# A fused retention and squared-ReLU kernel on one core: fixed rows of operations for each engine in place of a greedy list

## The chip, the cores and the metric

The kernel runs on one core of one Trainium2 chip. The metric is the device time of one execution in microseconds, given as the median of several runs of the same program. The profile is a separate look: one execution, recorded by the hardware profiler, whose span runs from the first to the last instruction. Engines are named as in the profile: PE (TensorE, matrix products; PEld is its loading of weights), DVE (VectorE), ACT (ScalarE), POOL (GpSimd) and SP (SyncE, which issues nearly all transfers).

## What is computed

```python
def _attn_ref(q, k, v):                       # 4 x 8 x 768 x 64 each, float32
    gamma = 1.0 - 2.0 ** (-5.0 - np.arange(H))
    for t in range(S):
        state = gamma * state + k_t (outer) v_t          # 64 x 64 for each batch and head
        y[:, :, t] = (1 / np.sqrt(D)) * (q_t @ state)

def _moe_ref(x, w_in, w_out):                 # x: y as 3072 tokens x 512
    h = np.maximum(x @ w_in, 0.0)             # 3072 x 2048
    return h * h @ w_out                      # 3072 x 512
```

A recurrence over 768 steps in 32 heads gives 3072 tokens of 512 numbers; a feed-forward layer with a squared ReLU follows.

## The kernel before

**Tiles.** The tokens are cut into 24 tiles of 128, six to a batch; tile m is the unit of everything below. Inside a tile the recurrence is done as two chunks of 64 with matrix products: scores of q and k under a mask, sums of k and v into the running state, values from the scores, and the state applied to q. The powers of gamma are folded into v beforehand and into the result afterwards. The inputs are float32, the products bfloat16.

**Operations.** The program is a list of named operations, each added by `pl.add` with its engine, a planned duration and what it reads and writes. The names are used throughout:

- `ldq`, `ldk`, `ldv` m: transfers of tile m, 256 KB each (512 KB for tiles 0 and 2, which are loaded as pairs), issued by SP (L537, L717). `ldwin0` to `ldwin3` are 512 KB pieces of w_in, `ldwin4`, `ldwin5` and `ldwout0` to `ldwout3` pieces of 1 MB (L910). The text calls the loads q9, k9, v9 and so on for short. Four buffers of each of q, k and v are held.
- `cq`, `ck`: casts to bfloat16, on DVE, ACT or POOL (L518 to L522). `cv`: the scaling of v (L728 on DVE, L553 for the pairs). `cwin`, `cwout`: casts of weight blocks.
- `X` m, from tile 7 on: a DMA transpose issued by SP (L761), which turns the cast q and k of the tile (`kqs`) into `qkT`. Earlier tiles are transposed on PE (`T`, evacuated by `E`).
- `A`, `B`, `C` (tiles 0 to 3, in pairs) and the visits `V` on PE. `V9.10` computes the values of tile 9 (L787, L802) and, in the same stretch, the scores and sums of tile 10 (L813, L824), so it needs X10 and the scaled v10. `P` (mask), `S` n.0 and n.1 (state) and `Y` (result into `xt`) are its operations on DVE.
- `F1` b.f on PE (L936): a group of products of block b, two tiles wide (one for b = 2 and 3), with part f of w_in, eight matmuls of 256 columns or sixteen of 128. `R` (ReLU, ACT, L943) empties its PSUM bank, `Q` (square, ACT or DVE, L950 and L952) writes `h`.
- `F2` t.j (L1108): the second layer for tiles 0 to 3, evacuated by `O` and stored by `st0` to `st3`. Tiles 4 to 23 take the second layer in pairs with seven products instead of eight, `M1` to `M7` (L1032), named by the first tile of the pair. DVE makes sums of blocks of h for them (L1007; `S1`, `S2`, `S5`, `S6`, `S7` before and `H1` to `H7` after the change) and of w_out (`WT`, L982); `e4`, `cc` on ACT (L1054, L1060) and `t`, `u`, `w`, `c` on DVE (L1050) read the products from two banks; `st4.0`, `st4.1` and so on store them (L1084, 256 KB each).

**Buffers that tie them.** Four PSUM banks `fps` are shared by F1, F2, M and T; two more pairs (`sc`, `yy`) serve the visits. R and Q share two buffers. Three output buffers (`osb`) and one more (`wu`) pass from store to store, so a result can be written only when the store before it from the same buffer has landed.

**What sets the order.** `Plan.schedule` (L68) runs when the program is built. It keeps a planned clock for every engine, the PSUM banks, the DMA stream and the fetching of instructions, and places one operation at a time: of all that are ready, the one that can start earliest, then the one with the lowest priority number (`prio`, overridden by the table `RANK`, L316). Operations that several engines could do go to the one that could start first, unless the table `HOME` (L277) says which. The sequence that comes out is emitted in order of planned start, so that each engine's instructions have a fixed order on the chip; waits between engines are semaphores that the framework adds. The order of the loads is a priority too (`ORDER`, L340). PE begins with 20 tiny matmuls and, in gaps before 20 us of the plan, gets fill matmuls (`ident`), 36 in all, that keep it busy while it waits.

The lines that choose:

```python
key = (t, o["prio"], i)
if best is None or key < best[0]:
    best = (key, i, eng)
```

Of the kernel before, what the change touches and what calls it, by code (L numbers as in the profile page):

```python
# [11 lines left out]
BF16 = mybir.dt.bfloat16  # L12
# [6 lines left out]
class Plan:  # L19
# [14 lines left out]
    HOP = 0.15  # L34

# [5 lines left out]
    def add(self, name, eng, dur, reads=(), writes=(), fn=None, prio=0.0, lat=0.0, bank=None, after=(), count=0, slot=None, lock=()):  # L41
# [22 lines left out]
        self.ops.append(dict(i=i, name=name, eng=eng, flex=flex, deps=sorted(deps), fn=fn,  # L64
                             prio=prio, lat=lat, bank=bank, count=count, slot=slot, lock=lock))
        return i

    def schedule(self, nbanks, max_open, nslots):  # L68
# [12 lines left out]
        for o in ops:  # L81
            for e in o["eng"]:
                eng_free.setdefault(e, 0.0)
                pool.setdefault(e, set())
                if left[o["i"]] == 0:
                    pool[e].add(o["i"])
# [15 lines left out]
        while done < n:  # L102
            best = None
            for eng, cand in pool.items():
                ef = eng_free[eng]
                for i in cand:
# [21 lines left out]
            (t, _, _), i, eng = best  # L128
            o = ops[i]
            for e in o["eng"]:  # L130
                pool[e].discard(i)
# [34 lines left out]
            else:  # L166
                if eng == "PE":
# [21 lines left out]
                    if any(before < x <= issued for x in range(self.BLOCK0 - self.AHEAD, issued + 1, self.BLOCK)):  # L189
# [14 lines left out]
                end[i] = t + dur + o["lat"]  # L204
# [15 lines left out]
            for u in users[i]:  # L220
                same = list(ops[u]["eng"]) == [eng] and not move
                ready_at[u] = max(ready_at[u], start[i] + dur if same else end[i] + self.HOP)
                left[u] -= 1
                if left[u] == 0:
                    for e in ops[u]["eng"]:
                        pool[e].add(u)
# [11 lines left out]
AHEAD = 4  # L238
WARM = 20.0
FILL = 0.215  # L240
WARMING = 18.4
PACE = 8
LEAD = 2
# [5 lines left out]
CVT = {'DVE': 0.69, 'POOL': 1.07}  # L249
TCAST = {'DVE': 0.43, 'ACT': 0.63, 'POOL': 0.64}  # L250
TEVAC = {'ACT': 0.6, 'DVE': 0.62}
NPAIR = 2
F2LAG = 3.5
F2WAIT = 4
LAST = [256, 128, 128]
CAST = {"k": {"DVE": 0.43, "ACT": 0.63, "POOL": 0.64}, "q": {"DVE": 0.43, "ACT": 0.63, "POOL": 0.64}}
WCAST = {"DVE": 0.43, "ACT": 0.63, "POOL": 0.64}
EVAC = {"ACT": 0.6, "DVE": 0.62}
WPRIO = {"in": -2.0, "out": 2.0, "sum": 3.0}
# [3 lines left out]
SQUARE = {"DVE": 0.7, "ACT": 0.63}  # L263
WSUM = {"DVE": 0.69}
ASUM = {"DVE": 0.69}
LAGS = {
    16: 4.0, 4: 10.75, 6: 18.25, 10: 2.25, 20: 1.75, 14: 3.0, 8: 2.25, 18: 3.0, 12: 1.75, 22: 2.0,
}
RELU = {"ACT": 0.6}
# [4 lines left out]
PAIRS_A = {"S1": ((0, 0), (1, 1), ALU.add, None), "S5": ((0, 0), (0, 1), ALU.add, None),  # L274
           "S2": ((1, 0), (1, 1), ALU.add, None), "S6": ((1, 0), (0, 0), ALU.subtract, (1, 0)),
           "S7": ((0, 1), (1, 1), ALU.subtract, (0, 1))}
HOME = {  # L277
# [36 lines left out]
}  # L314
ROUND = []
RANK = {  # L316
# [36 lines left out]
def kernel(  # L353
# [638 lines left out]
    def products(c0):  # L992
# [31 lines left out]
        def product(i, bank, half, bank_use):  # L1024
# [13 lines left out]
            if first:  # L1038
                op["op"] = pl.ops[k]
# [168 lines left out]
```

## Time and profile before

| | before |
|---|---|
| median of 3 runs | 203.87 us |
| the runs | 203.72, 203.87, 205.05 us |
| span of the profiled execution | 202.7 us |
| time of that execution around its span | not in the page; the median run is 1.2 us longer than the span |
| granted clock of PE | 1.000 |
| busy: PE, PEld | 192.8 us (95%), 159.4 us (79%) |
| busy: DVE, ACT, POOL | 150.0 us (74%), 130.3 us (64%), 31.3 us (15%) |
| transfers | 97,935 packets, 38.46 MB, mean 190 GB/s |

The profile page lists busy times, the span in 40 slices of 5.07 us (a digit is the busy share in tenths, 9 for 90% or more), the DMA queues, the chain of work that ended last, the costliest groups of instructions, and the transfers. Other views of the same trace show single instructions in time with the idle time ahead of each and what released it, waits summed by who waited for whom, and busy times in chosen stretches. A busy PE is not PE at its peak: the ends of matmuls are modelled, so the distance between starts tells more than the durations.

### The profile page before, as it was taken

The page shows a single profiled execution, that of the slowest core. Times are in us where ns is not written, and L with a number is a line of the kernel's source. Part 1 is how long each engine was busy: PE and PEld are TensorE (multiplying, and loading weights), DVE is VectorE, ACT ScalarE, POOL GpSimd, SP SyncE. Part 2 cuts the span into 40 slices and gives each one's busy share as a digit, 9 for nine tenths or more (in the row PEclk, how much of TensorE's full clock was granted, in tenths as well). Part 3 has the DMA queues.
Part 4 walks back from the last instruction along what each step waited for, and adds up shares of the span by engine and source line. Part 5 has one row for each costly group of instructions (what it writes and reads, how often), then busy time and mean ns, then how long its engine had stood idle before and what let it go on. Part 6 is the DMA issues. An engine that isn't in the chain of part 4 may idle for free.

```text
span 202.7 us, 7020 instructions
## 1 busy us (share of the span) xinstructions
PE 192.8 (95%) x3032; PEld 159.4 (79%) x3032; DVE 150.0 (74%) x283; ACT 130.3 (64%) x229; POOL 31.3 (15%) x56
## 2 busy tenths in 40 slices
PE   8886999899989999999999999999999999999992
PEld 6554887664577888888888888888888888888881
DVE  3486449569849988969898888878998784934762
ACT  8565888788871883787975485569375873835210
POOL 6541252220102101310211012203010000000000
PEclk9999999999999999999999999999999999999999
DMA  5999999999999999999999999999676100111313
GB/s 159 290 314 320 348 344 330 361 246 210 236 191 219 231 247 212 205 234 186 148 240 165 261 211 218 178 222 194 143 145 97 48 17 3 52 52 55 102 55 105
DMA packets 97935, 38.46 MB, mean 190 GB/s; under 512 B 81008, under 2 KB 94320, under 8 KB 97904
## 3 DMA queue, kind: packets, MB, share of 16 engines
q1 hardware_dynamic: 97760, 37.89, 86.2%
q8 instruction: 23, 0.38, 0.8%
q10 hardware_dynamic: 144, 0.13, 0.2%
q14 instruction: 8, 0.07, 0.1%
HBM read 27.26 MB, written 6.29 MB: 166 GB/s over the span
## 4 chain that ended last, share of the span: by engine, by line
PE 75%; DMA 15%; SPq 5%; POOL 1%; DVE 1%; issue 1%; ACT 0%; DVEq 0%
PE fps L936 33%; PE fps L1032 29%; DMA kn<-in_k_dram 8%; PE fps L1108 6%; DMA wst<-in_moe_w_in_dram 4%; DMA qkT<-kqs 3%; SPq L910 3%; PE yy L787 2%; SPq L537 2%; PE yy L802 1%; PE sc L813 1%; PE sc L824 1%; POOL w_in L522 1%; DVE wu L1050 1%; POOL h L522 0%
## 5 line engine op out<-in xcount | busy, mean ns | idle before, releaser
L936 PE MATMUL fps<-xt,w_in 128*128 128x256 bf16 (+1 forms) x832 | 94.0, 264 | 1.6 <-ACT w_in L518 1.2
L936 PEld LDWEIGHTS <-w_in 128*128 128x128 bf16 x832 | 74.8, 98 | 11.5 <-ACT w_in L518 2.0
L943 ACT ACTIVATE r<-fps 128x512 f32<-128x512 f32 x96 | 56.4, 592 | 34.6 <-PE fps L936 28.6
L950 ACT ACTIVATE h<-r 128x512 bf16<-128x512 f32 x63 | 39.1, 627 | 1.4
L1032 PE MATMUL fps<-wst,h 128*128 128x256 bf16 x320 | 39.4, 273 | 0.0
L1032 PEld LDWEIGHTS <-h 128*128 128x128 bf16 x320 | 31.0, 98 | 3.9
L952 DVE TENSOR_TENSOR h<-r 128x512 bf16<-128x512 f32 x33 | 22.8, 705 | 8.7 <-ACT r L943 8.6
L1032 PEld LDWEIGHTS <-wst 128*128 128x128 bf16 x240 | 23.3, 98 | 2.8
L1007 DVE TENSOR_TENSOR wst<-h 128x1024 bf16<-128x1024 bf16 x30 | 19.4, 685 | 2.9 <-ACT h L950 2.6
L1032 PE MATMUL fps<-w_out,wst 128*128 128x256 bf16 x160 | 20.3, 273 | 0.0
L728 DVE TENSOR_TENSOR vs<-vn,vf 128x512 bf16<-128x512 f32 x20 | 13.8, 691 | 6.3 <-DMA vn<-in_v_dram 6.3
L889 DVE TENSOR_TENSOR xt<-yy,yf 128x512 bf16<-128x512 f32 x20 | 13.7, 687 | 3.5 <-PE yy L802 3.4
L522 POOL CAST kqs<-kn 128x512 bf16<-128x512 f32 x12 | 8.0, 666 | 51.0 <-DMA kn<-in_k_dram 32.3
L1108 PE MATMUL fps<-w_out,h 128*128 128x512 bf16 x64 | 15.0, 379 | 0.7 <-DVE w_out L520 0.7
L1007 DVE TENSOR_TENSOR h<-h 128x1024 bf16<-128x1024 bf16 x20 | 14.0, 729 | 0.2
L880 DVE TENSOR_TENSOR state<-sc,state 128x256 bf16<-128x256 f32 x33 | 13.8, 418 | 0.5
L867 DVE TENSOR_TENSOR pt<-sc,cmask 128x512 bf16<-128x512 f32 x20 | 13.6, 681 | 0.0
L522 POOL CAST kqs<-qn 128x512 bf16<-128x512 f32 x11 | 6.9, 626 | 42.9 <-DMA qn<-in_q_dram 30.6
L1050 DVE TENSOR_TENSOR wu<-fps,wu 128x512 f32<-128x512 f32 (+1 forms) x16 | 9.1, 572 | 5.0 <-ACT osb L1060 2.8
L1108 PEld LDWEIGHTS <-h 128*128 128x128 bf16 x64 | 5.9, 98 | 6.8 <-issue 0.8
L1060 ACT ACTIVATE osb<-fps 128x512 f32<-128x512 f32 x10 | 5.9, 594 | 8.3 <-PE fps L1032 8.3
L1050 DVE TENSOR_TENSOR osb<-fps,osb 128x512 f32<-128x512 f32 (+1 forms) x15 | 9.0, 601 | 2.6 <-PE fps L1032 1.7
(85 smaller groups left out, 173.4 us busy)
## 6 DMA issues: line engine op xcount, KB each, us to landing
qn<-in_q_dram SPq DMA_DIRECT2D x20, 256.0 KB, 5.1
kn<-in_k_dram SPq DMA_DIRECT2D x20, 256.0 KB, 5.6
vn<-in_v_dram SPq DMA_DIRECT2D x20, 256.0 KB, 5.2
out_dram<-osb SPq DMA_DIRECT2D x19, 256.0 KB, 3.3
wst<-in_moe_w_out_dram SPq DMA_DIRECT2D x4, 1024.0 KB, 10.1
wst<-in_moe_w_in_dram SPq DMA_DIRECT2D x4, 512.0 KB, 8.4
wst<-in_moe_w_in_dram SPq DMA_DIRECT2D x2, 1024.0 KB, 8.3
kn<-in_k_dram SPq DMA_DIRECT2D x2, 512.0 KB, 4.3
```

What stands on the lines that cost most here:

```text
L522: nc.gpsimd.tensor_copy(o, t)
L728: lambda: nc.vector.tensor_tensor(out=o[:], in0=t.rearrange("s (h d) -> s h d", h=H), in1=vf[:, i, :, None].to_broadcast([P, H, D]), op=AL ...
L880: f = lambda cc=cc, j1=j1, j0=j0: nc.vector.tensor_tensor(out=sts[j1][:], in0=cc, in1=sts[j0][:], op=ALU.add)
L889: lambda: nc.vector.tensor_tensor(out=xt[:, :, u * C : u * C + C].rearrange("s p (g t) -> s g p t", g=2), in0=yy[:, :, 0:256].rearrange("s ...
L936: nc.tensor.matmul(ps[:, u * n : u * n + n], lhsT=w_in_bf[j][:, cb, c * P : (c + 1) * P], rhs=xt[:, cb, cols], start=(cb == 0), stop=(cb = ...
L943: nc.scalar.activation(o, t, AF.Relu)
L950: nc.scalar.activation(hv, rv, AF.Square)
L952: (nc.vector if on == "DVE" else nc.gpsimd).tensor_tensor(out=hv, in0=rv, in1=rv, op=ALU.mult)
L1007: lambda on, o=a[name], x=a[x], y=a[y], op=op: (nc.vector if on == "DVE" else nc.gpsimd).tensor_tensor(out=o, in0=x, in1=y, op=op), prio=c ...
L1032: nc.tensor.matmul(ps[:, 256 * half : 256 * half + 256], lhsT=a[left][:, f], rhs=right(f), start=(first and f == 0), stop=True, skip_group ...
L1050: return lambda ps: nc.vector.tensor_tensor(out=o, in0=ps[:, lo:hi], in1=y, op=op)
L1108: nc.tensor.matmul(ps[:, 0:w], lhsT=h2[:, fb, u * C : u * C + C], rhs=w_out_bf[j][:, c, ns], start=(fb == 0), stop=(fb == NFB - 1))
```

## The change

The arithmetic, the tiles, the buffers and the instructions are the same; PE has 3,032 matmuls in both. What changes is who decides the order and the engine.

- The tables `HOME`, `RANK`, `ORDER`, `LAGS` and all priorities are gone. A table `TURNS` has for each of the five engines one row of names, which holds every operation once. `schedule` still runs its planned clock (for the choice of PSUM banks and buffers, the fill matmuls and the order of emission), but an engine's only candidate is the next name of its row.
- The planned durations are cut (a DVE pass 0.69 to 0.602, a cast on ACT 0.63 to 0.52, and so on) and a tail is added to an operation's end (`TAIL`). An effect of instruction fetching on loads is planned only before 55 us (`LATE`).
- Some operations on PE are tied to others by `after`: F1 of a block of h to the openers of the group two before, and the first M of a bank to the one before.
- A double visit, `visit2`, is added; with `DOUBLE = 24` it is reached for the last visit alone, which does what it did.
- The sums of blocks of h are renamed `S1` to `H1` and so on.

```diff
+    LATE = 55.0
+    TAIL = {"DVE": 0.08, "ACT": 0.11, "POOL": 0.055}
...
-        if name in HOME:
-            eng = {HOME[name]: eng[HOME[name]]}
-        prio = RANK.get(name, prio)
...
+        turns = {e: [known[x] for x in TURNS[e].split()] for e in pool}
+        for e, x in turns.items():
+            for i in x:
+                ops[i]["eng"] = {e: ops[i]["eng"][e]}
+        at = dict.fromkeys(pool, 0)
+
+        def offer():
+            for e, x in turns.items():
+                if at[e] < len(x) and left[x[at[e]]] == 0:
+                    pool[e].add(x[at[e]])
...
-                    key = (t, o["prio"], i)
-                    if best is None or key < best[0]:
-                        best = (key, i, eng)
+                    if best is None or t < best[0]:
+                        best = (t, i, eng)
...
-                    if any(before < x <= issued for x in range(self.BLOCK0 - self.AHEAD, issued + 1, self.BLOCK)):
+                    if t < self.LATE and any(before < x <= issued for x in range(self.BLOCK0 - self.AHEAD, issued + 1, self.BLOCK)):
...
-                end[i] = t + dur + o["lat"]
+                end[i] = t + dur + o["lat"] + self.TAIL.get(eng, 0.0)
...
+TURNS = {
+    "POOL": ( "ident iota3 iota iota2 cmask2 cmask cq0.1 ck2.1 ...
+    "DVE": ( "lng ex2_f ex_f lnt vf ck0.1 ck0.0 vf2 Ek0.0 cv0.0 cv0.1 P0.00 ...
```

The rows that come out, as both programs issue them, in the stretches that matter (before above, after below):

```
SP, first loads
  k0 q0 v0 q2 k2 v2 win0 win1 win2 q4 win3 win4 k4 win5 v4 wout0 q5 wout1 k5 wout2 wout3 q6 v5 k6 v6 q7 k7 v7 k8 q8 st0 st1 X7 v8 k9 X8
  k0 q0 v0 k2 q2 v2 win0 win3 q4 win1 win2 win4 k4 win5 v4 wout0 wout1 wout2 q5 k5 wout3 k6 v5 k7 q6 q7 v6 q8 k8 v7 X7 v8 k9 X8
SP, then up to v19
  st2 q9 v9 k10 q10 v10 st3 X9 k11 q11 v11 X10 st4.1 k12 q12 v12 X11 st4.0 k13 q13 v13 X12 k14 q14 X13 st6.1 v14 k15 q15 X14 v15 k16
    q16 X15 st6.0 v16 k17 q17 v17 X16 st8.1 k18 X17 st8.0 q18 v18 k19 q19 v19
  q9 st2 st0 q10 v9 k10 k11 v10 X9 st3 v11 q12 X10 q11 v12 k12 k13 v14 q13 X11 st1 k14 X12 k15 k16 q14 v13 st4.0 X13 v15 q15 k18 X14
    st4.1 q16 st6.0 k17 X15 v16 v18 X16 q19 q17 k22 k19 q18 v17 q20 X17 q21 v20 X18 q22 k21 st6.1 st8.1 k20 X19 v19
PE, from F1.0.0
  F1.0.0 F1.0.2 C2.0 C2.1 F1.0.4 Tq4 F1.1.0 F1.0.6 F1.1.2 F1.1.4 F1.1.6 F1.0.8 Tk4 F1.0.10 F1.1.8 F1.1.10 V.4 F1.0.12 ...
  F1.0.0 F1.0.6 C2.0 C2.1 F1.0.2 Tq4 F1.1.0 F1.1.6 F1.0.4 F1.1.2 F1.1.4 F1.0.10 Tk4 F1.0.8 F1.1.8 F1.1.10 F1.0.12 V.4 ...
PE, around V8.9 and V9.10
  V7.8 M4.4 M1.4 F1.4.0 F1.4.2 M5.4 F1.4.4 F1.4.6 M2.4 F1.4.8 V8.9 F1.4.12 F1.4.10 F1.4.14 M3.6 M6.4 M7.4 V9.10
  V7.8 F2.3.3 M4.4 F1.4.6 F1.4.4 M1.4 F1.4.0 F1.4.14 M5.4 F1.4.2 V8.9 M2.4 F1.4.8 F1.4.12 M6.4 V9.10
PE, around V18.19
  V17.18 F1.8.10 M1.12 F1.8.12 F1.8.14 M4.12 F1.9.0 F1.9.8 M5.12 V18.19
  V17.18 F1.8.2 M5.10 M2.10 F1.8.8 M3.12 M4.12 M6.10 V18.19
PE, the end
  M3.22 M4.22 M6.20 M7.20 M1.22 M5.22 M2.22 M7.22 M6.22
  M3.22 M4.22 M6.20 M7.20 M5.22 M2.22 M1.22 M6.22 M7.22
DVE, two stretches of the row after
  V11.12's: P12 ck16 cq14 u1.6 S12.1 ck14 cv13 w.6 H1.8 c.6
  V17.18's: Q8.10 ck20 P18 cv19 w.10 H1.14 P19 t1.12 H5.14 Y18 c.10 S19.0
```

These operations change engine:

| operations | from | to |
|---|---|---|
| 24 squares Q | ACT | DVE |
| 22 squares Q | DVE | ACT |
| 2 scalings cv (tile pair 0) | POOL | DVE |
| casts of q, k and weights | | DVE +16, ACT -12, POOL -4 |
| 4 evacuations E | DVE | ACT |
| 1 copy of a state, S0 | ACT | DVE |

More of the change, by code (lines that the diff above doesn't have):

```diff
@@ L39, in __init__, with add @@
         self.readers = {}
-    def add(self, name, eng, dur, reads=(), writes=(), fn=None, prio=0.0, lat=0.0, bank=None, after=(), count=0, slot=None, lock=()):
+    def add(self, name, eng, dur, reads=(), writes=(), fn=None, lat=0.0, bank=None, after=(), count=0, slot=None, lock=()):
         i = len(self.ops)
@@ L84, in schedule @@
                 pool.setdefault(e, set())
-                if left[o["i"]] == 0:
-                    pool[e].add(o["i"])
+        known = {o["name"]: o["i"] for o in ops}
+        turns = {e: [known[x] for x in TURNS[e].split()] for e in pool}
+        assert sorted(i for x in turns.values() for i in x) == list(range(n))
+        for e, x in turns.items():
[6 more added lines that the diff above has]
+                    pool[e].add(x[at[e]])
+        offer()
         if "PE" in eng_free:
@@ L221, in schedule @@
                 same = list(ops[u]["eng"]) == [eng] and not move
-                ready_at[u] = max(ready_at[u], start[i] + dur if same else end[i] + self.HOP)
+                ready_at[u] = max(ready_at[u], (start[i] + dur if eng not in self.TAIL else end[i] + 0.01) if same else end[i] + self.HOP)
                 left[u] -= 1
-                if left[u] == 0:
-                    for e in ops[u]["eng"]:
-                        pool[e].add(u)
+            offer()
         self.start, self.end, self.on = start, end, [o["on"] for o in ops]
@@ L248 @@
 WHALFD = (0.60, 1.47, 33, 0.6)
-CVT = {'DVE': 0.69, 'POOL': 1.07}
-TCAST = {'DVE': 0.43, 'ACT': 0.63, 'POOL': 0.64}
-TEVAC = {'ACT': 0.6, 'DVE': 0.62}
+CVT = {'DVE': 0.602, 'POOL': 1.003}
+TCAST = {'DVE': 0.338, 'ACT': 0.52, 'POOL': 0.558}
+TEVAC = {'ACT': 0.48, 'DVE': 0.5}
 NPAIR = 2
-F2LAG = 3.5
 F2WAIT = 4
 LAST = [256, 128, 128]
[L256 to L259, printed above, removed]
+CAST = {"k": {"DVE": 0.338, "ACT": 0.52, "POOL": 0.558}, "q": {"DVE": 0.338, "ACT": 0.52, "POOL": 0.558}}
+WCAST = {"DVE": 0.338, "ACT": 0.52, "POOL": 0.558}
+EVAC = {"ACT": 0.48, "DVE": 0.341}
 BOTH = ("DVE", "POOL")
[L263 to L269, printed above, removed]
+SQUARE = {"DVE": 0.602, "ACT": 0.52}
+WSUM = {"DVE": 0.602}
+ASUM = {"DVE": 0.602}
+RELU = {"ACT": 0.48}
 APART = (22,)
@@ L273 @@
            "T6": ((0, 0), (0, 1), ALU.add), "T7": ((1, 0), (1, 1), ALU.add)}
[L274 to L277, printed above, removed]
[36 rows of a table removed]
-}
-ROUND = []
-RANK = {
[22 rows of a table removed]
-}
-ORDER = (
-    "k0 q0 v0 q2 k2 v2 i0 i1 i2 q4 i3 i4 k4 i5 v4 o0 q5 o1 k5 o2 o3 q6 v5 k6 v6 q7 k7 v7"
-)
-def dma_order(nm):
-    names = {"i": "in", "o": "out"}
-    seq = [(names.get(t[0], t[0]), int(t[1:])) for t in ORDER.split()]
-    return seq + [(x, m) for m in range(nm) for x in "kqv" if (x, m) not in seq]
+PAIRS_A = {"H1": ((0, 0), (1, 1), ALU.add, None), "H5": ((0, 0), (0, 1), ALU.add, None),
+           "H2": ((1, 0), (1, 1), ALU.add, None), "H6": ((1, 0), (0, 0), ALU.subtract, (1, 0)),
+           "H7": ((0, 1), (1, 1), ALU.subtract, (0, 1))}
+TURNS = {
+    "POOL": (
+        "ident iota3 iota iota2 cmask2 cmask cq0.1 ck2.1 cq2.1 cq2.0 cv2.0 cwin0.2 cwin3.2 cwin2.0 ck4 cwout2.3 "
+        "ck5 cwout2.0 cwout3.0 cwout3.3 cq6 ck6 cq8 cq9 cq10 cq11 cq13 cq15 ck18 cq16 cq17 ck19 cq19 cq18 cq21 "
+        "cq22 ck21 cq20 ck22 ck23 cq23 "
+    ),
+    "DVE": (
[15 rows of a table added]
+    ),
+    "ACT": (
[12 rows of a table added]
+    ),
[8 rows of a table added]
+    ),
[16 rows of a table added]
+    ),
+}
 @with_exitstack
@@ L681, in add_up @@
                     nc.vector.tensor_tensor(out=sts[j1][:], in0=cc, in1=sts[j0][:], op=ALU.add)
-            pl.add(f"S{m + c}", {"DVE": 0.42, "ACT": 0.45} if first else "DVE", 0.42, (f"gB{m + c}",) if first else (f"gB{m + c}", f"S{j0}"), (f"S{j1}",), add_up,
-                   prio=urgency(m) - 0.5, bank=("close", ("B", m + c)))
+            pl.add(f"S{m + c}", {"DVE": 0.341, "ACT": 0.28} if first else "DVE", 0.341, (f"gB{m + c}",) if first else (f"gB{m + c}", f"S{j0}"), (f"S{j1}",), add_up, bank=("close", ("B", m + c)))
         for b2 in range(2):
@@ L703, in out_fn @@
                                         in1=f, op=ALU.mult)
-            pl.add(f"Y{m}.{b2}", "DVE", 0.68, banks[b2] + (f"yf{b2}", f"yf{2 + b2}"),
-                   [f"xt{g % NXT}.{u + c}" for c in range(2)], out_fn, prio=urgency(m))
+            pl.add(f"Y{m}.{b2}", "DVE", 0.602, banks[b2] + (f"yf{b2}", f"yf{2 + b2}"),
+                   [f"xt{g % NXT}.{u + c}" for c in range(2)], out_fn)
     def prepare(m):
@@ L881, in visit @@
                         out=sts[j1][:], in0=cc, in1=sts[j0][:], op=ALU.add)
-                pl.add(f"S{n}.{sub}", "DVE", 0.42, (f"sc{sub}",) if first else (f"sc{sub}", f"S{j0}"), (f"S{j1}",), f,
-                       prio=urgency(n))
+                pl.add(f"S{n}.{sub}", "DVE", 0.341, (f"sc{sub}",) if first else (f"sc{sub}", f"S{j0}"), (f"S{j1}",), f)
         if m is not None:
@@ L887, in visit @@
             xt = xts[g % NXT]
-            pl.add(f"Y{m}", "DVE", 0.68, ("yy0", "yy1") + tuple(f"yf{p}" for p in range(NJ)), (f"xt{g % NXT}.{u}",),
+            pl.add(f"Y{m}", "DVE", 0.602, ("yy0", "yy1") + tuple(f"yf{p}" for p in range(NJ)), (f"xt{g % NXT}.{u}",),
                    lambda: nc.vector.tensor_tensor(
@@ L1069, in products @@
             product(7, "B", 0, "use")
[L1070 removed]
+            read("c", "DVE", 0.602, "B", kwu, kwu, on_psum(wu[:], 0, 512, wu[:], ALU.subtract), close=True)
         if last:
@@ L1078, in products @@
                         out[rows(c0) + lo * C : rows(c0) + lo * C + C, col : col + 256], wu[:, 256 * lo : 256 * lo + 256])
-                pl.add(f"st{c0}.{lo}", "ACT" if lo == 0 else "SP", STORE, k, (), f, prio=-1)
+                pl.add(f"st{c0}.{lo}", "ACT" if lo == 0 else "SP", STORE, k, (), f)
             return
@@ L1141 @@
         n = m + 1
-        for x in range(0 if m < 0 else m + AHEAD, min(NM, m + AHEAD + 1)):
+        if n > DOUBLE:
+            xs = range(prepared, min(NM, n + AHEAD) if n % 2 else prepared)
+        else:
+            xs = range(0 if m < 0 else m + AHEAD, min(NM, m + AHEAD + 1))
+        for x in xs:
             prepare(x)
             transpose(x)
+            prepared = x + 1
         t = m + 2 if NPE <= m + 2 < NTD else None
-        if n < 2 * NPAIR:
+        if n >= DOUBLE:
+            if n % 2 == 0:
+                visit2([x for x in (n - 2, n - 1) if n > DOUBLE or x == n - 1], [x for x in (n, n + 1) if x < NM])
+        elif n < 2 * NPAIR:
             if n % 2 == 0:
```

275 lines of the change are left out of this document (156 added, 119 removed), and 109 rows, old and new, of tables (HOME, RANK, TURNS).

## The prediction

> **What bounds the kernel now.** I read the page first: span, busy shares, the DMA row.
>
> ```profile
> span 202.7 us, 7020 instructions
> ...
> PE   8886999899989999999999999999999999999992
> ...
> DMA  5999999999999999999999999999676100111313
> ```
>
> Two things are full at once: TensorE from the fifth slice to the last but one, and the DMA engines until slice 30, about 150 us. The clock row is 9 throughout, so the clock plays no part. The busy table by stretches, read next, has PE 20.00 of 20.00 us in 90 to 110, 110 to 130 and 130 to 150, and DVE between 17.16 and 18.21 there. So the question is where PE still loses time, and whether the DMA stream leaves room to win it. The PE timeline answers the first (start, length, engine, instructions, in brackets the idle time before and its releaser):
>
> ```profile
> 17.54 1.35 PE L936 MATMUL fps<-xt,w_in 128*128 128x256 bf16 x8 [1.03 <-ACT w_in L518]
> 19.05 1.05 PE L936 MATMUL fps<-xt,w_in 128*128 128x256 bf16 x8 [0.16 <-ACT w_in L518]
> ...
> 58.39 0.32 PE L813 MATMUL sc<-qkT 64*64 64x64 bf16 x16 [0.53 <-DMA qkT<-kqs]
> ...
> 62.87 0.32 PE L813 MATMUL sc<-qkT 64*64 64x64 bf16 x16
> ...
> 134.92 0.32 PE L787 MATMUL yy<-pt,vs 64*64 64x64 bf16 x16
> ...
> 197.03 1.91 PE L1032 MATMUL fps<-wst,h 128*128 128x256 bf16 x16
> ```
>
> I turn this into a clock of PE's work. A group of eight 128x256 matmuls (F1 or M) passes every 0.873 us when nothing stands in its way (the merged rows, 24 of them in 2.62 us), an F2 group takes 0.864, a one-tile F1 group 0.93, and a visit 0.67 plus 0.1 for the slower start of its neighbour, taken as 0.78. Work ahead of an operation, counted from the first F1 group, subtracted from its start gives an offset. It is 17.5 at the start, 18.3 at 21.36 us, 19.6 at V6.7 (57.48), 20.2 at V7.8 (62.42), and 20.4 from V8.9 (71.28) to V22.23 (160.69). So PE loses 2.9 us before 63 us and nothing after it. The row order cannot shorten the work itself: both rows hold the same 228 operations and the same 36 warm-up matmuls. All that can be won is this loss.
>
> **The part that can be won.** The first 0.8 us stays: F1.0.0 waits for the first w_in piece, seventh load in both rows, and the second group for the eighth. After the C2 pair the new row runs F1.0.2, whose piece is now loaded behind q4: the second piece lands at 18.35, q4 takes 1.1 and a piece 1.5 (the w_in casts on ACT that waited for DMA start at 16.86, 18.36 and 19.90), so 20.95, plus the cast 0.63 and a handoff: 21.65 instead of 21.36, +0.3. From there two stalls go. F2.0.1 idled 0.68 at 39.05 for its w_out cast; w_out 1 now lands before q5, at about 36, and F2.0.1 stands at 40.3. V6.7 waited 0.53 at 58.39 for a transpose; stores st0 and st1 stood ahead of X7 and now stand behind it. With nothing late anywhere PE keeps offset 21.65 - 3.09 = 18.56 against 20.37: -1.8 us. That is the ceiling, 0.9%. The tail is the same length: the last two products trade places, two 0.42 us evictions and one store follow.
>
> **The part that moves between engines.** DVE gets 2 squares, 2 v scalings, 16 casts and one state copy, and gives 4 evacuations: 2 x 0.71 + 2 x 0.69 + 16 x 0.42 + 0.42 - 4 x 0.45 = +8.1 us; ACT gives some 6.7, POOL 4.6. I cost this at nothing: 158 us of DVE lie beside 193 of PE. Where the cover is thinnest, 90 to 110 us, DVE has 1.8 us to spare; a late operand that blocks its row longer than this reaches PE.
>
> **The part that decides: loads and visits.** The new rows put the late visits earlier among PE's work (V9.10 by three groups, V18.19 by five: F1.9.0, F1.9.8, M1.12, M5.12 and M7.10 come behind it), and SP's row puts other loads first. Up to v19, which V18.19 needs, seven loads (q20, k20, v20, k21, q21, k22, q22) and two transposes (X18, X19) are moved ahead of it, and one store behind. What the stream delivers is seen on POOL, whose casts start when their load lands:
>
> ```profile
> 60.63 0.61 POOL L522 CAST kqs<-kn 128x512 bf16<-128x512 f32 x1 [9.10 <-DMA kn<-in_k_dram]
> 64.45 0.61 POOL L522 CAST kqs<-qn 128x512 bf16<-128x512 f32 x1 [3.20 <-DMA qn<-in_q_dram]
> 66.77 0.69 POOL L522 CAST kqs<-kn 128x512 bf16<-128x512 f32 x1 [1.71 <-DMA kn<-in_k_dram]
> ...
> 83.55 0.98 POOL L522 CAST kqs<-kn 128x512 bf16<-128x512 f32 x1 [3.43 <-DMA kn<-in_k_dram]
> 84.72 0.61 POOL L522 CAST kqs<-qn 128x512 bf16<-128x512 f32 x1 [0.19 <-DMA qn<-in_q_dram]
> 90.41 0.61 POOL L522 CAST kqs<-qn 128x512 bf16<-128x512 f32 x1 [5.08 <-DMA qn<-in_q_dram]
> ...
> 122.34 0.61 POOL L522 CAST kqs<-qn 128x512 bf16<-128x512 f32 x1 [3.73 <-DMA qn<-in_q_dram]
> 124.44 0.61 POOL L522 CAST kqs<-kn 128x512 bf16<-128x512 f32 x1 [1.49 <-DMA kn<-in_k_dram]
> 129.10 0.61 POOL L522 CAST kqs<-qn 128x512 bf16<-128x512 f32 x1 [4.04 <-DMA qn<-in_q_dram]
> ...
> 138.93 0.61 POOL L522 CAST kqs<-kn 128x512 bf16<-128x512 f32 x1 [1.54 <-DMA kn<-in_k_dram]
> 139.99 0.61 POOL L522 CAST kqs<-qn 128x512 bf16<-128x512 f32 x1 [0.45 <-DMA qn<-in_q_dram]
> ```
>
> These are k9, q9, k10, k13, q13, q14, q19, k20, q20, k22, q22. Neighbours give a load: 1.1 us (139.99 - 138.93, and 2.10 for two at 122.34). A store is as large as a quarter of a 1 MB weight load; those land 2.82 us apart (ACT's w_in casts at 22.57 and 25.39), so 0.7. From k9 to q22 pass 79.36 us, 40 loads, 10 stores and 13 transposes: (79.36 - 44 - 7) / 13 = 2.2 us a transpose on average. Single stretches give 1.6 (66.77 to 83.55: 9 loads, 3 stores, 3 transposes) to 2.9 (124.44 to 129.10).
>
> Now the new row. k9 lands two stores earlier, 60.63 - 1.4 = 59.2. From k9 to v19 stand 39 loads, 9 stores, 12 transposes: 42.9 + 6.3 + 12X. The cast is then first in DVE's row (0.69); PE asks for it 0.45 us into V18.19. That visit stands at 110.2 us of work, so the offset cannot be under 59.2 + 49.2 + 12X + 0.24 - 110.2 = 12X - 1.6. V9.10 stands at 54.3 and needs X10, which is three transposes (X8 to X10), 8 loads and 3 stores behind k9: 59.2 + 8.8 + 2.1 + 3X = 70.1 + 3X; scores start 0.35 into the visit, so its offset is at least 15.45 + 3X. V8.9 (50.0) needs X9, two transposes, 6 loads and 2 stores behind k9: at least 16.85 + 2X. At X = 2.2 the bounds of V18.19 and V9.10 are 24.8 and 22.1; at 1.9, 21.2 and 21.2; at 1.6, 17.6 and 20.3. I take 1.9. The dear stretches have SP itself waiting for the casts that a transpose reads:
>
> ```profile
> SPq L761 <- POOL kqs L522: 9.8, 5, 3.3
> SPq L761 <- ACT kqs L518: 5.8, 2, 5.5
> ```
>
> and the new row fetches k and q several places earlier, so part of these waits should go, but not all: 1.9 is halfway from the mean to the cheapest stretch.
>
> [...]
>
> **Sum.** Offset 21.2 against 20.4: +0.8 us. 202.7 + 0.8 = 203.5 us of span; the median run, 203.87, lies 1.2 over the profiled span, whose own total the page does not give, so 204.7. The early gain of 1.8 is real in this forecast, but it is given back in waits for X9 and X10 and again at v19. PE will be late next at V18.19; behind the blocked cast on DVE are queued w.10, H1.14, P19 and t1.12, whose delay V19.20 and the bank of unit 10 feel.
>
> **Rivals.** *Late v19 (slower).* The stream keeps its mean of 2.2 us: offset 24.8, +4.4, 208.3. It decides as soon as v19 lands after 130.3. For it: PE's row now asks for a tile every 5.9 us between V5.6 and V22.23 (99.9 us of work over 17 visits, 6.3 before), and three loads, a store and a transpose cost 3.3 + 0.7 + 2.2 = 6.2. Against it: SP's waits above can only shrink.
>
> *Cheap transposes (faster).* Issued at 143.76, when little else is queued, a transpose takes 3.3 us to land where a lone store (177.10) takes 2.1 (the DMA issues of those moments): 1.2 us more. If that is its whole cost, and the rest of the 2.2 is waiting for casts, V18.19 and V9.10 are bound under 19.1, V8.9 at 19.25, and the offset ends there: -1.1, 202.7. Against it: the lone store's 2.1 holds its own 0.7, which would make the transpose 1.9. [...]
>
> *Nothing moves.* The old row too was fixed when the program was built, by a greedy pass over planned times; on the chip both are plain in-order rows. If the visits after V8.9 stay where the loads let them, losses and gains cancel: 203.9.
>
> *Blocked rows.* DVE now holds casts that wait for loads (ck8, ck16, cq14, cv13, cv17, cv19) with bank-releasing reads behind them, which ACT could wait for without harm before. Two such blocks over 1.8 us in the DVE-full stretch add to a late v19: past 208.4.
>
> **Numbers.** About 2 us, 1%, is what a measurement here can tell from no change (the three runs span 203.72 to 205.05). Forecast (203.6 to 205.9) 0.43, late v19 (206 to 208.4) 0.28, cheap transposes (202.0 to 203.5) 0.14, nothing moves 0.10, blocked rows 0.05. Slower by over 1% is over 205.9: 0.28 + 0.05 and 0.03 of the forecast's edge, 0.36. Faster by over 1% lies beyond the ceiling and needs an error in my work clock: 0.05. The rest, 0.59, is within 1%. The range 202.2 to 208.0 leaves out the blocked rows, the end of the late case and what is beyond the ceiling.
>
> **What would show it.** F1.0.2 starting at 21.65; no wait near 39 or at V6.7; the offset rising to 20.5 or more at V8.9 and V9.10 with PE waiting for a transpose; PE or DVE waiting for v19 at V18.19; a mean transpose between 1.8 and 2.0. An offset still at 18.6 after V18.19 would make the cheap transposes right, one of 23 or more the late v19. Waits of PE on DVE or ACT where no load is late would show a cause that I left out.

## The result, and the profile after

| | before | after |
|---|---|---|
| median | 204.46 us (4 runs, 203.72 to 206.00) | 211.55 us (4 runs, 211.33 to 212.06) |
| ratio | | 1.0321, interval 1.0254 to 1.0387 |
| profiled execution: span, own time | 202.7 us | 209.7 us, 211.52 us |

The change makes the kernel 3% slower: 7.0 us between the two spans. The page first, the rows that were shown of before (busy tenths in 40 slices, now of 5.24 us):

```profile
span 209.7 us, 7020 instructions
...
PE   8687899997999679999999869999999999999993
...
PEclk9999999999999999999999987999999999999999
DMA  5999999999999999999999999999411011011223
```

PE has three dents that it did not have: slice 10 (47 to 52 us), slices 14 and 15 (68 to 79 us) and slices 23 and 24 (115 to 126 us). Behind the last the granted clock falls too (its digits are 8 and 7 in slices 24 and 25). The DMA row is as full as before up to slice 28. PE's waits, summed by what they waited for (total us, times, longest), name the second dent, and with their second row a part of the third:

```profile
PE sc L788 <- DMA qkT<-kqs: 4.2, 4, 1.8
PE fps L973 <- DVE osb L1088: 1.3, 1, 1.3
```

Before, the first of these rows was 0.5 us in one wait. PE's timeline shows where they are (start, length, engine, instructions, in brackets the idle time before and its releaser):

```profile
71.74 0.32 PE L788 MATMUL sc<-qkT 64*64 64x64 bf16 x16 [1.80 <-DMA qkT<-kqs]
...
77.67 0.32 PE L788 MATMUL sc<-qkT 64*64 64x64 bf16 x16 [1.51 <-DMA qkT<-kqs]
...
119.62 1.91 PE L973 MATMUL fps<-xt,w_in 128*128 128x256 bf16 x16 [0.55 <-ACT r L980]
122.78 1.03 PE L973 MATMUL fps<-xt,w_in 128*128 128x256 bf16 x8 [1.25 <-DVE osb L1088]
...
124.81 0.43 PE L788 MATMUL sc<-qkT 64*64 64x64 bf16 x16 [0.69 <-DMA qkT<-kqs]
...
125.49 1.89 PE L1067 MATMUL fps<-wst,h 128*128 128x256 bf16 x8
```

These are the scores of V8.9 (waiting for X9), of V9.10 (X10), two F1 groups, the scores of V16.17 (X17), and an M group of eight matmuls that takes 1.89 us where others take 1.04: the granted clock is 0.5 from 124.69 to 128.10 us. The second of the two F1 groups waits for a bank that VectorE empties, and its timeline says why it is late:

```profile
117.73 0.41 DVE L853 TENSOR_TENSOR state<-sc,state 128x256 bf16<-128x256 f32 x1
121.10 0.69 DVE L706 TENSOR_TENSOR vs<-vn,vf 128x512 bf16<-128x512 f32 x1 [2.96 <-DMA vn<-in_v_dram]
121.71 0.42 DVE L853 TENSOR_TENSOR state<-sc,state 128x256 bf16<-128x256 f32 x1
122.04 0.68 DVE L1088 TENSOR_TENSOR osb<-fps,osb 128x512 f32<-128x512 f32 x1
122.64 0.68 DVE L841 TENSOR_TENSOR pt<-sc,cmask 128x512 bf16<-128x512 f32 x1
```

S16.0, then cv17 at the head of the row, idle for 2.96 us until v17 has landed, and behind it S16.1, c.8 (which empties the bank) and P16. The first F1 group's 0.55 us has the same form on a smaller scale: cv16 and cv18 waited 0.76 and 0.55 us for their loads at 111, the square Q7.12 behind them came late, and a ReLU on ScalarE waited 2.68 us for the buffer that Q7.12 reads. On the prediction's clock (offset = start of an operation less the work ahead of it; that work is 50.0 us for V8.9, 110.2 for V18.19) this gives:

| offset at the start of | V7.8 | V8.9 | V9.10 | V10.11 | V15.16 | V16.17 | V17.18 | V22.23 |
|---|---|---|---|---|---|---|---|---|
| after | 19.5 | 19.6 | 21.5 | 23.2 | 23.5 | 25.6 | 27.9 | 27.9 |

Before it was 20.4 from V8.9 on. So PE is 0.8 us ahead of the old kernel at V8.9, loses 1.9 and 1.7 at X9 and X10, 2.1 behind these casts of v, 2.3 at X17 and in the half clock, and ends 7.5 behind.

### The profile page after: what moved, and what is told of

The parts are those of the page before. It is cut to its first block, busy times and chain, and to the rows that moved or that the text cites. A ratio compares the mean times of both kernels' runs of the same rounds, so it can differ in the third digit from the quotient of the medians.

```text
span 209.7 us, 7020 instructions
## 1 busy us (share of the span) xinstructions
PE 193.1 (92%) x3025; PEld 160.5 (77%) x3032; DVE 155.8 (74%) x300; ACT 122.3 (58%) x218; POOL 28.6 (14%) x50
## 4 chain that ended last, share of the span: by engine, by line
PE 51%; DMA 20%; SPq 13%; ACT 5%; DVE 5%; issue 2%; POOL 1%; DVEq 0%; POOLq 0%
PE fps L973 23%; PE fps L1067 22%; DMA qn<-in_q_dram 9%; DMA qkT<-kqs 6%; SPq L696 5%; DMA kn<-in_k_dram 5%; SPq L531 4%; ACT r L980 3%; SPq L738 2%; SPq L948 2%; PE fps L1146 2%; DVE wu L1088 1%; PE yy L762 1%; POOL kqs L516 1%; PE sc L788 1%
## 5 line engine op out<-in xcount | busy, mean ns | idle before, releaser
L973 PE MATMUL fps<-xt,w_in 128*128 128x256 bf16 (+1 forms) x832 | 93.0, 265 | 2.5 <-DVE osb L1088 1.3
L980 ACT ACTIVATE r<-fps 128x512 f32<-128x512 f32 x96 | 55.6, 594 | 45.1 <-PE fps L973 37.8
L987 ACT ACTIVATE h<-r 128x512 bf16<-128x512 f32 x61 | 37.3, 626 | 1.0
L1067 PEld LDWEIGHTS <-h 128*128 128x128 bf16 x320 | 31.3, 99 | 4.3
L989 DVE TENSOR_TENSOR h<-r 128x512 bf16<-128x512 f32 x35 | 25.3, 722 | 8.3 <-ACT r L980 8.2
L1067 PEld LDWEIGHTS <-wst 128*128 128x128 bf16 x240 | 23.2, 98 | 2.8
L1042 DVE TENSOR_TENSOR wst<-h 128x1024 bf16<-128x1024 bf16 x30 | 20.6, 695 | 4.0 <-PE fps L1067 2.9
L516 POOL CAST kqs<-qn 128x512 bf16<-128x512 f32 x15 | 10.5, 701 | 74.1 <-DMA qn<-in_q_dram 72.7
L1067 PE MATMUL fps<-w_out,wst 128*128 128x256 bf16 x160 | 19.6, 273 | 0.0
L1067 PE MATMUL fps<-wst,wst 128*128 128x256 bf16 x80 | 10.4, 273 | 0.0
L777 PE MATMUL yy<-qkT,state 64*64 64x64 bf16 x296 | 10.1, 198 | 0.2
```

Source lines behind the costliest of these rows:

```text
L973: nc.tensor.matmul(ps[:, u * n : u * n + n], lhsT=w_in_bf[j][:, cb, c * P : (c + 1) * P], rhs=xt[:, cb, cols], start=(cb == 0), stop=(cb = ...
L980: nc.scalar.activation(o, t, AF.Relu)
L987: nc.scalar.activation(hv, rv, AF.Square)
L989: (nc.vector if on == "DVE" else nc.gpsimd).tensor_tensor(out=hv, in0=rv, in1=rv, op=ALU.mult)
L1042: lambda on, o=a[name], x=a[x], y=a[y], op=op: (nc.vector if on == "DVE" else nc.gpsimd).tensor_tensor(out=o, in0=x, in1=y, op=op), lock=BOTH)
L1067: nc.tensor.matmul(ps[:, 256 * half : 256 * half + 256], lhsT=a[left][:, f], rhs=right(f), start=(first and f == 0), stop=True, skip_group ...
```

## The experiments

Three theories were put against each other. **Theory S:** the DMA stream as a whole sets the pace; TensorE's row asks for tiles faster than the stream delivers, so a transfer brought forward puts another one back. **Rival R:** a few misplaced loads cost what their waits show, and these add up. **Rival D:** the transfers are not the matter; the new order on VectorE and ScalarE and the moves between engines are. All ratios are to the kernel before, run beside them.

**The rows alone.** The old rows written into the new program:

```diff
-TURNS = { the changed rows }
+TURNS = { the five rows that the old pass gave }
...
-                       after=both_open[-1:] if first else ())
+                       after=())
```

> The new program text with all five rows filled with the order that the old greedy pass gave (and without the planner's one extra dependence between openings of M units, which that order does not keep). If the rows alone make the difference: 203.7 to 205, PE's offset 20.4 from V8.9 on, no half clock. If anything else in the new text costs time: towards 211.5.

Measured: 204.13 us, ratio 1.0005 (0.9989 to 1.0022); V22.23 starts at 160.30, before at 160.68. Nothing but the rows makes the difference. One thing came otherwise: this profile has a stretch of half clock from 19.02 to 22.43 us. Eleven of the fifteen profiles of this case have one before 22.5 us; those of the kernel before, the changed kernel, v17_early and fill17 have none. Here it is made good by V7.8 (62.36 us, before 62.42).

**X9 and X10 first.** One edit in SP's row:

```diff
-ldq9 st2 st0 ldq10 ldv9 ldk10 ldk11 ldv10 X9 st3 ldv11 ldq12 X10
+ldq9 st2 st0 ldq10 ldv9 ldk10 X9 ldk11 ldv10 X10 st3 ldv11 ldq12
```

> SP's row only: X9 moved ahead of the loads k11 and v10, X10 ahead of st3, v11 and q12. X9 then lands near 69.5 instead of 71.7, X10 near 74 instead of 77.6. Theory S (the DMA stream as a whole is what TensorE waits for; one repair moves the wait to the next late transpose): the waits of 1.80 and 1.51 us go, but X11 still lands at 84.9, X12 at 89.5 and X13 at 97.8, so TensorE waits some 2 us for X11 and the rest for X13, and the offset is 23.5 after V12.13 as before: 211.5, within 0.5. Rival R (each misplaced load costs its own wait and the waits add up): 3.3 us less, 208.2.

Measured: 211.73 us, ratio 1.0359 (1.0300 to 1.0418). Rival R is out: X9 landed at 70.1 and X10 at 73.2, neither is waited for, and nothing is won. The place of the new waits was not what I expected; they are not at X11 but behind casts that wait for loads: cv10 and cv11, whose loads were put back, cq14 (1.84 us of PE at 96.16), and ck10. k10 keeps its place, but with X9 right behind it it lands at 69.09 and not at 67.35. The timelines of this kernel, PE's and then ScalarE's:

```profile
70.33 1.03 PE L973 MATMUL fps<-xt,w_in 128*128 128x256 bf16 x8 [1.52 <-ACT r L980]
...
77.11 0.32 PE L762 MATMUL yy<-pt,vs 64*64 64x64 bf16 x16 [1.47 <-DVE xt L861]
```

```profile
69.17 0.63 ACT L512 ACTIVATE kqs<-kn 128x512 bf16<-128x512 f32 x1 [2.14 <-DMA kn<-in_k_dram]
69.70 0.58 ACT L980 ACTIVATE r<-fps 128x512 f32<-128x512 f32 x1
```

ck10 stands in ScalarE's row ahead of a ReLU that empties a bank; it waited 2.14 us for k10, and PE 1.52 us for the ReLU.

**v17 and cv17.** Two kernels, one edit each:

```diff
 SP (v17_early)
-X16 ldq19 ldq17 ldk22 ldk19 ldq18 ldv17 ldq20 X17
+X16 ldv17 ldq19 ldq17 ldk22 ldk19 ldq18 ldq20 X17
 DVE (cv17_later)
-S16.0 cv17 S16.1 c.8 P16 H5.12
+S16.0 S16.1 c.8 P16 cv17 H5.12
```

> SP's row only: v17 moved five places ahead, to stand behind X16. It lands near 115.6 instead of 121.1, so cv17 on VectorE no longer waits 2.96 us and c.8 and P16 come in time. Theory S: V16.17 reaches its scores 2 us earlier and waits there for X17 (124.8) instead, in one idle of about 2 us; v19 (136.2) then holds V18.19 at an offset near 26.3; only what the half clock took (1.7 us) comes back, if it does: 209.8 to 211.5. Rival R (the blocked row on VectorE costs 2.1 us and the half clock that follows 1.7, both gone with it): 207.5 to 208. In both, the clock row tells whether the half clock hangs on the stall at 119 to 123.

> VectorE's row only: cv17 moved behind S16.1, c.8 and P16; the loads stay. S16.1, c.8 and P16 no longer stand behind the wait for v17. If the head-of-row wait was the cause of TensorE's idles of 0.55 and 1.25 us, these go, the same as with an early v17, and by theory S X17 takes the wait over: 209.8 to 211.5. By rival R: 207.5 to 208. If late v17 itself was the cause (H and P behind it still late), no change and the idles stay in their place: 211.5.

Measured: 210.98 us, ratio 1.0348 (1.0310 to 1.0386), and 210.93 us, ratio 1.0347 (1.0295 to 1.0400). Both took the wait for c.8 away, and in both PE then waited for X17 in one piece. PE's timeline of the first, with the F1 group that follows at half clock:

```profile
123.49 0.32 PE L788 MATMUL sc<-qkT 64*64 64x64 bf16 x16 [2.17 <-DMA qkT<-kqs]
...
124.81 1.70 PE L973 MATMUL fps<-xt,w_in 128*128 128x256 bf16 x8
```

In the second the wait is 2.63 us. Theory S had 209.8 to 211.5, rival R 207.5 to 208. The half clock stayed, so it does not hang on cv17; an idle of PE there is what is left to try.

**The idle filled.** v17_early, and 14 matmuls of no use inside the wait for X17:

```diff
             if n is not None:
+                for _ in range(14 if n == 17 else 0):
+                    nc.tensor.matmul(sc[:, 0, 0 : 2 * P], lhsT=ident[:], rhs=ident[:, None, :].to_broadcast([P, 2, P]),
+                                     start=True, stop=True, skip_group_check=True)
                 scores(n)
```

> v17_early with 14 matmuls of 128x256 on the identity put into V16.17, ahead of the scores that wait for X17: some 1.5 us of work (14 x 0.109) inside the idle of 2.17 us. If the half clock at 125.0 to 128.4 hangs on that idle, the clock stays full there and 1.7 us come back: 209.2 against 210.98. If the clock falls by itself, the time stays at 211.0; if the fills push work on the path, it is above.

Measured: 210.00 us, ratio 1.0226 (1.0161 to 1.0290). Between the medians that is 1.0 us less than v17_early, between the ratios 1.2% or 2.5 us, so the runs alone do not give the size. The profile does. Its clock row and the lines of PE's timeline:

```profile
PEclk9999999999999999999999999999999999999999
```

```profile
122.21 1.70 PE L826 MATMUL sc<-ident 128*128 128x256 bf16 x14
124.15 0.32 PE L788 MATMUL sc<-qkT 64*64 64x64 bf16 x16 [0.24 <-DMA qkT<-kqs]
...
136.73 0.32 PE L800 MATMUL sc<-vs,kqs 64*64 64x64 bf16 x16 [0.28 <-DVE vs L706]
```

The clock stays full, and from the first score of V16.17 to the start of V17.18 pass 4.90 us (124.15 to 129.05) instead of 6.57 (123.49 to 130.06): 1.67 us for one stretch of half clock. Then the last line: V18.19 now waits for the scaled v19, as the prediction's bound for it says, and the offset ends at 26.3 (V22.23 starts at 159.65; in v17_early at 160.10, an offset of 26.7). The two profiles differ ahead of the edit, where V16.17 starts 0.95 us later in fill17 (121.89 against 120.94), so their ends do not show the whole 1.67.

**The stream relieved.** If S holds, rows and engines can stay and the time must fall when the stream has less to carry. Two ways:

```diff
 small_stores
-                           out[rows(q4) : rows(q4) + C, ns], osbs[slot][:, ns]))
+                           out[rows(q4) : rows(q4) + z, ns], osbs[slot][0:z, ns]))
 (with z = 8, and the pair stores of chunks 4, 6 and 8 likewise)
 half_x
-  nc.sync.dma_start_transpose(out=qkT.rearrange("p x j t -> p (x j) t"), in_=t.rearrange("s x j a d -> s (x j a d)"))
+  nc.sync.dma_start_transpose(out=qkT[:, 0:1].rearrange(...), in_=t[:, 0:1].rearrange(...))
```

> The changed kernel with all rows as they are, but the result stores of the first chunks (st0 to st3, st4, st6, st8 of both halves) write 8 of their 128 tokens, so the rest of those output rows is left unwritten. Nine such stores lie between k9 and v19 in SP's row, 0.7 us of the stream each. Theory S (the stream sets the pace): X9 lands 1.4 earlier, X10 2.1, X13 3.5, X17 5.6 and v19 6.3; the waits at 71.7 and 77.7 shrink to about 0.4 and 0.8, those at 119 to 125 and the half clock there go; final offset about 20.8, 204.4 us. Rival D (the order on VectorE and ACT and the engine moves cost the time, not the transfers): the waits of TensorE stay, 210 to 211.5.

> The changed kernel with all rows as they are, but each DMA transpose from X8 on turns the k half of its tile and leaves q as it was from an earlier tile (scores and products with q are then of stale data). If a transpose costs the stream by its bytes, 2.35 us falls to about 1.2, v19 lands up to 13 us earlier, no visit waits, and the offset ends at 19.5 to 20: 203 to 203.8. If a transpose costs by its issue on SP (about 2 us of SP each, whatever its size), the landings stay and so does the time: 210 to 211.5.

Measured: 205.34 us, ratio 1.0032 (0.9984 to 1.0080), and 205.69 us, ratio 1.0047 (1.0004 to 1.0090). Six of the seven microseconds come back with no row and no engine changed. PE's waits of small_stores, which before its edit were 4.2 and 1.3:

```profile
PE sc L788 <- DMA qkT<-kqs: 1.1, 3, 0.5
```

V22.23 starts at 155.09, an offset of 21.7 where 20.8 was expected; X17 landed at 120.04, 4.7 us earlier, which is 0.7 for each of the seven cut stores ahead of it. half_x, whose edit halves X7 too, missed its 203 to 203.8: a half transpose is far dearer than half. Its k9 lands at 59.63 and v19 at 131.75; less 39 loads of 1.1 and 9 stores of 0.7 that leaves 1.9 us for each of twelve half transposes, where the whole ones took 2.3 in the changed kernel and 2.2 in v17_early. So v19 came 4.5 us earlier and not 13, and neither of the two prices in the expectation, by bytes or by issue alone, holds. One wait for X9 (1.04) and one behind c.8 (1.19) stayed.

**The same relief for the old rows**, the stores cut as in small_stores:

> The old five rows, with the early result stores cut to 8 of 128 tokens as in small_stores (st0 to st3, st4, st6, st8; the rest of those output rows is left unwritten). If the old rows wait for nothing in the stream after 63 us, as PE's flat offset of 20.4 says, relief changes nothing: 203.5 to 204.5. If the old rows too are paced by the stream, they gain what the relief gave the changed rows, up to 3 us: 201 to 202.5.

Measured: 204.07 us, ratio 0.9986 (0.9956 to 1.0016). No gain. The old rows do not wait for the stream; the new ones do.

**The engine moves alone.** The old rows, with 51 operations given to the engines that the change gives them:

> The old rows, but the 51 casts and squares from tile 8 and unit 4 on that the change gives to another engine are done by that engine, each put into its row by its old planned start; loads, PE's row and all else stay. The prediction costed the engine moves at nothing: 204 to 204.6. If operands that come from a fuller VectorE are what TensorE waits for, part of the 7 us shows here: 206 or more.

Measured: 205.70 us, ratio 1.0070 (1.0041 to 1.0098), 1.2 us over its neighbours' 204.50. Neither end: not nothing. ScalarE's and then PE's timeline:

```profile
66.34 0.63 ACT L512 ACTIVATE kqs<-kn 128x512 bf16<-128x512 f32 x1 [4.53 <-DMA kn<-in_k_dram]
66.88 0.36 ACT L1092 ACTIVATE e<-fps 128x256 f32<-128x256 f32 x1
```

```profile
67.75 1.03 PE L1067 MATMUL fps<-w_out,wst 128*128 128x256 bf16 x8 [1.44 <-DVE osb L1088]
```

By these rows it is not the busy time that was moved. ck10, which GpSimd could wait for with nothing behind it, now waits for k10 at the head of ScalarE's row; the copy e of a product stands behind it, a sum on VectorE behind that, a bank behind that. (My rows put it there by the old planned times; in the changed kernel the same cast waits 0.79 us and PE does not feel it.)

**Only the transfers reordered.** TensorE's row, the engine of every operation and the order of all that is no load, transpose, store or cast of q, k, v are the change's; the rest was moved by a search over small steps, with a transpose priced higher in the planned clock. Two kernels; the second keeps the change's loads up to q9. Around X16:

```diff
 SP (loads_only)
-X16 ldq19 ldq17 ldk22 ldk19 ldq18 ldv17 ldq20 X17 ldq21 ldv20 X18 ldq22 ldk21 st6.1 st8.1 ldk20 X19 ldv19
+X16 ldk22 ldv17 ldq18 ldq19 X17 ldv18 ldk19 X18 st6.0 ldk20 ldv19 st6.1 X19
```

> The changed kernel, in which only loads, transposes, stores and the casts of q, k and v change their places (each cast in its own engine's row); TensorE's row, the engine of every operation and the order of all others are the change's. v17 stands behind X16 and cv17 behind P16; ahead of v19 stand 35 loads, 7 stores and 11 transposes from k9 on, not 39, 9 and 12. By 1.1, 0.7 and 2.3 us each v19 lands some 8 us earlier, near 128; X9 still near 71.5, X10 near 76. Theory S: one wait of 1 to 2 us for X9 stays, the later ones, the stall behind cv17 and the half clock at 125 go; final offset 21 to 22.5, 204.5 to 206.5. Rival D (TensorE's row and the moves of evacuations between engines are the loss): 209 to 211.5.

> As loads_only, but SP's row up to q9 is the change's own, and only loads, transposes and casts of tiles 9 and up, and stores, change their places behind it; TensorE's row and all other operations stand as in the change. Ahead of v19 stand 33 loads, 6 stores and 11 transposes from k9 on: 59.4 + 36.3 + 4.2 + 25.9 = 125.8 instead of 136.2; X9 near 71.0, X10 near 76.3, X13 near 96.1, X17 near 120. If the order of the loads is the whole loss: offset 19.6 at V8.9 as in the change, a wait of 1.1 us for X9 and of 0.8 for X10 at most, then level; 21 to 22 at V22.23, 204 to 205.5. If the changed TensorE row or the engine moves have a price of their own behind 72 us: 206.5 or more, with waits for VectorE or ScalarE after 80 us.

Measured: 208.09 us, ratio 1.0160 (1.0110 to 1.0209), and 210.30 us, ratio 1.0228 (1.0171 to 1.0286). Both miss upwards. In loads_only the mechanism is there: v19 landed at 126.5 and no visit from V8.9 on waits for a transpose. PE's timeline at V8.9:

```profile
72.24 0.32 PE L762 MATMUL yy<-pt,vs 64*64 64x64 bf16 x16
...
72.45 0.30 PE L788 MATMUL sc<-qkT 64*64 64x64 bf16 x16
```

V8.9 starts at 72.24 and V22.23 at 156.60: offsets of 22.2 and 23.2, so 1.0 us is lost between the two where the change lost 8.3. What spoils the total is an offset that is already 2.7 higher at V8.9, from new waits for ScalarE ahead of it (1.32 us at 44.06 the longest); 0.6 of the 2.7 stand there already at V4. (35.03, in the changed kernel 34.39), behind a stretch of half clock at 18.5 us that the changed kernel's profile does not have. late_loads was to take just those waits away, and did not pay either. Its profile is of the longest of its six runs, 213.27 us where the others took 208.12 to 210.82, so its sizes are not those of the median. No visit in it waits for a transpose. It shows short waits (1.02 us for an output copy at 66.16, 0.85 for a scaled v at 96.79) and a long one, VectorE's line first and then PE's:

```profile
145.41 0.69 DVE L706 TENSOR_TENSOR vs<-vn,vf 128x512 bf16<-128x512 f32 x1 [6.27 <-DMA vn<-in_v_dram]
```

```profile
147.45 3.27 PE L973 MATMUL fps<-xt,w_in 128*128 128x256 bf16 x16 [4.36 <-ACT r L980]
```

cv21 at the head of VectorE's row waits for v21, a square behind it, a ReLU on ScalarE behind that, a bank behind that, and half clock follows from 147.80 to 151.21. How much of this the other five runs have is not known. The time and these waits meet the expectation's second case, a price of TensorE's row or of the engine moves; but the long wait is for a load, so they do not decide.

**All rows searched anew.** The same search over all rows, from the change's and from the old ones:

> The changed kernel's five rows, searched anew from where they stood by small moves of single operations in all rows, with one thing altered in the planned times that the search minimises: a DMA transpose takes the stream 1.6 to 2.4 us (three such plans, their mean is minimised) instead of the 1.10 us of the table TURN; the chip's landings from k9 to v19 ask for 2.3 (76.9 us, less 39 loads of 1.1 and 9 stores of 0.7, over 12). Theory S: with an honest price of the stream the same kind of search gives rows that do not wait for transposes: 203.5 to 205.5. If the loss has another root than the price of the transposes, it stays near 209 to 211.

> The same search with the same prices, started from the old greedy rows. By theory S the old rows already keep pace with the stream, so there is little to win: 203.2 to 204.2 against 204.1 to 204.4, at best half a percent. If the old rows had been far from what the stream allows, 201 to 203.

Measured: 208.33 us, ratio 1.0207 (1.0155 to 1.0260), and 213.20 us, ratio 1.0388 (1.0336 to 1.0440). The first recovers 3.2 us and PE waits for no DMA transpose in it, but it loses elsewhere; the second turns rows that kept pace into the slowest of all. Its VectorE and PE:

```profile
130.75 0.43 DVE L514 CAST kqs<-kn 128x512 bf16<-128x512 f32 x1 [4.48 <-issue]
```

```profile
133.03 1.03 PE L973 MATMUL fps<-xt,w_in 128*128 128x256 bf16 x8 [2.68 <-DVE wu L1088]
```

A cast of k at the head of the row again (ck19; k19 lands at 130.67), 4.48 us without work, a bank release behind it, and half clock from 134.03 to 137.44. A better price of the transposes alone does not give good rows. No version tried beats the kernel before.

## Why the prediction went wrong

**What bounds the kernel.** Right: PE and the stream are full at once, and the question was what the stream leaves room for. old_small and small_stores show it from both sides.

**The part that can be won.** Half right. The stalls of F2.0.1 and at V6.7 went as said. The ceiling of 18.56 was not reached: F1.0.2 started at 22.00 instead of 21.65, and moving q6 behind v5 and k7 made a wait that I had not looked for (its cast on GpSimd, 1.22 us of PE at 50.67). At V8.9 the gain was 0.8 us and not 1.8.

**The price of a transpose: the step that failed.** I took 1.9 us. In the changed kernel k9 lands at 59.38, X10 at 77.62 and v19 at 136.23. With my own 1.1 and 0.7 for loads and stores that is (18.24 - 8.8 - 2.1) / 3 = 2.45 up to X10 and (76.85 - 42.9 - 6.3) / 12 = 2.3 up to v19. The long stretch is the one to go by: in v17_early and fill17, with nothing altered up to X10, the same sums give 1.7 and 2.0 up to X10, but 2.2 and 2.3 up to v19. The reason for going under the mean of 2.2 was that SP's waits for casts would shrink. In part they did; the largest row of SP's waits at transposes is now

```profile
SPq L738 <- POOL kqs L516: 6.5, 3, 3.9
```

in place of 9.8 and 5.8. All rows of such waits together went from 18.6 (these two and 3.0 put down to another operation) to 14.6 us (this one, 4.1, 2.7 and 1.3), and the transposes became no cheaper. What makes the price stays open: from k9 to v19 SP's queue was held by its transfers, part of the waits included, for 72.0 of the 76.85 us, 27.9 of them by twelve transposes, while the DMA row is full as well; half_x, with 1.9 us for half the bytes, says only that it is not the bytes alone. With 2.3 my bound for V18.19 is 26.0; fill17, with little else in the way, ended at 26.3. So the formula held and one term was too small: by 0.4 in X times 12, some 5 of the 7 us. The place was not the one I named: in the changed kernel V18.19 does not wait, because the waits for X9, X10 and X17, the casts of v and the half clock had put PE at 27.9 by V17.18, above that bound. My rival *Late v19* had this mechanism and 208.3.

**Why the plan liked it.** The planned clock in the program has X10 at 72.3, v19 at 127.0 and the end at 202.3 for the new rows, 204.0 for the old. The chip's landings are 5.3 and 9.2 us later, the lag growing from 2.2 at k9. That too low a stream price is in it (1.10 us for a transpose in the table `TURN`) is argued from these times; again shows that correcting it helps by 3 us and is not all.

**Blocked rows.** I gave this 0.05 and named cv17 among the casts. cv17 made the largest single stall, 2.96 us of VectorE, but no loss of its own: v17_early and cv17_later took it away, and X17 kept nearly all of it. In x9x10, old_dve, again_b and the profile of late_loads the same form, a cast waiting for its load at the head of a row with a bank release behind, cost PE 1.4 to 4.4 us each. I had priced this form too low.

**Engine moves at nothing.** Not shown to be nothing: old_dve cost 1.2 us in its arrangement, through one such cast and not through VectorE's busy time. With the stream relieved, the changed rows are at 205.34, so moves and order together can hold little over 1 us there.

**What I left out.** The granted clock. I wrote that it plays no part; 1.7 us of the 7 are a stretch of half clock, 3.41 us from 124.69 on, that follows PE's idles of 1.25 and 0.69 us.

**What stays open:** whether a row of TensorE with visits as early as the change has them can be fed at all. loads_only and late_loads took the waits for transposes away and met others; neither settles it.

## What to carry to other kernels

When a stream is full, read an order of transfers as a sum up to the first thing that is needed (with 2.3 us a transpose the sum put V18.19 at an offset of 26.0, and fill17 ended at 26.3), and price each kind by its landings over a long stretch where the stream is full. Do not count on waits of the issuing queue as a part of that price that can be saved: here they shrank from 18.6 to 14.6 us, and a transpose went from 2.2 to 2.3. Moving one load ahead only chooses who waits next, which relief of the stream (shorter stores, 205.34 us here) tells from a bad order in one run. In a fixed row a cast that waits for a load belongs where nothing that frees a bank stands behind it; here such casts cost PE 1.4 to 4.4 us each.

## What the hardware showed that I had not expected

In mid-kernel the clock fell behind PE idles of 1.8 to 3.1 us. A stretch of half clock there lasts 3.41 us: 124.69 to 128.10 in the changed kernel, 134.03 to 137.44 in again_b, 147.80 to 151.21 in late_loads. I count PE's idle in the 3.41 us just ahead of it, a choice of mine: 3.07 us in late_loads, 2.63 in cv17_later, 1.99 and 2.41 in again_b, 1.89 in v17_early (of a wait of 2.17) and 1.82 in the changed kernel (the 1.25 and most of the 0.69). The longest single wait that stayed without effect in mid-kernel is 1.84 us, in x9x10 at 96.16. All of these carry the error of matmul ends that are modelled. Idle time alone is not the measure: ahead of 19 us, among small matmuls, half clock followed 1.13 us of idle in old_dve (waits of 0.8 and 0.3) and did not follow 1.39 in the changed kernel (0.23 and 1.16, ahead of 15.74 and 17.25). What else counts was not tried.

The stream is not the same from run to run: X10, with nothing altered ahead of it, landed at 77.6, 75.6 and 76.2 us in the profiles of the changed kernel, v17_early and fill17. The waits for X9 and X10 that the changed kernel's profile shows are therefore one case of several.
